# Third tile's weights loaded through POOL's queue, and the second block's last rows of x rounded before the first two evictions

## The chip, the cores and the metric

The kernel runs on one core of a Trainium2 chip. The metric is the device time of one execution in microseconds, as the median of several runs. The kernel before took 900.96 us (three runs, 900.55 to 901.79).

## What is computed

Two attention branches over one input x of 2048 positions by 448 features, in float32, 16 heads of 28 features each, mixed by a gate:

```python
def reference(A_x, A_wqkv, A_wo, B_x, B_wqkv, B_wo, gate_w):
    x = A_x
    g = _sigmoid((x * gate_w).sum(-1, keepdims=True))
    a = _A_ref(x, A_wqkv, A_wo)   # each position attends to itself and 7 earlier ones, 2 apart
    b = _B_ref(x, B_wqkv, B_wo)   # full attention: softmax(q k^T / sqrt(28)) v over all 2048 positions
    return g * a + (1 - g) * b
```

Each branch starts with a product of x with its 448 by 1344 matrix `wqkv` and ends with one with its 448 by 448 matrix `wo`. The change lies in the first microseconds of the first of these products.

## The kernel before

**Tiles and precision.** A float32 product is made of three products of rounded numbers: each operand is split into a rounded high part (ScalarE, a copy into the type float32r) and the rest (a subtraction on VectorE or GpSimd), and high times high, low times high and high times low are added up in PSUM. The names are `xh` and `xl` for x, `wh` and `wl` for weights, `raw`, `wr` and `wt` for weights as loaded, and `V` for x as loaded (the tile that later holds v serves as the landing place). x is laid out with its 448 features along the partitions, as three groups of 128 (`kt` 0 to 2) and a last group of 64 rows, the *tail* (`kt` 3), whose low part lies in the other 64 partitions of the same tile. It is cut into four blocks of 512 positions.

**The opening.** Queries and keys of the full attention are projected first, in tiles of 128 features by 512 positions. Tiles 0 and 1 take block 0 with two slices of the weights (`wa`, columns 128 to 383 of the set); tile 2 takes block 0 with a third slice (`wb`, the first 128 columns), which has loads of its own: `wr1` (384 rows, 192 KB, L413) and the tail half of `wt0` (twice 64 rows, 32 KB each, L414 through L234). Tile 3 is the first that takes block 1. Tiles 0 and 1 are interleaved so that TensorE can follow the arrival of the pieces (`FIRST`, L300); from tile 2 on a tile is eleven matmuls in the order of L298: four of high by high, four of high x by low weights, three of low x by high weights. Nine matmuls on zeros (L217) run ahead of all that.

**What sets the order.** The order of each engine's work is the order in which the code is written (a manual schedule). The loads of the opening are written at L408 to L419: the first weights and, through ScalarE's queue, the three groups of block 0; then, all through SyncE's queue, the tail of block 0, the tail half of the weights, `wr1`, the rest of the tail half, the tail of block 1 (L415), the three groups of block 1 (L416), block 2, the tails of blocks 2 and 3, block 3. Each DMA counts on one of eight semaphores in turn, and a DMA that reuses one waits for the DMA eight places earlier. GpSimd fills two key tiles with ones (L82) and then has nothing to do until the second weight set.

**ScalarE and VectorE in the opening.** After block 0 and its weights they split `wt0` and `wr1` for tile 2 (L437 to L439, through L228 and L229), evict tiles 0 and 1 from PSUM (L361 and L362), then split block 1 (`split_x(1)`, written behind tile 1 at L482): its tail first (L259, L260), and then its three groups (L228, L229). Evicted tiles are stored to DRAM (L99) and read back later.

**After the opening.** The projections of v and of the other branch follow, with the first pass of the full attention (S1: row maxima) mixed in between from tile 11 on; the main loop then runs over 16 groups of queries and heads by 16 key tiles, with the sliding attention on GpSimd and VectorE beside it; the output projection ends the kernel.

Of the kernel before, what the change touches and what calls it, by code (L numbers as in the profile page):

```python
# [25 lines left out]
def gated_mix_kernel(ctx: ExitStack, tc: tile.TileContext, xT, xn, gw, wA, wB, woAB, out):  # L26
    nc = tc.nc
# [61 lines left out]
    def ptile(name):  # L89
        if name[0] == "w":  # L90
            return pair(name)[:, 0, :]
        h = half.setdefault(name[:2], [])
        if not h:
            t = pair(name)
            h.extend((t[:, 1, :], t[:, 0, :]))
        return h.pop()
# [5 lines left out]
    def load_k(g, t, src, c=slice(0, S)):  # L102
        for h in range(4):
            r = D + 112 * g + DH * h
            dma_r(t[32 * h:32 * h + DH, c], src[r:r + DH, c])
# [114 lines left out]
    with tc.tile_pool(name="xp", bufs=1) as xp, tc.tile_pool(name="wp", bufs=2) as wp:  # L220
# [3 lines left out]
        def raw3():  # L224
            return wp.tile([128, 3, 450], F32, tag="raw", name="raw", bufs=2)

        def split(hi, lo, raw, eng=nc.vector):
            nc.scalar.activation(hi, raw, AF.Copy)  # L228
            eng.tensor_tensor(out=lo, in0=raw, in1=hi.bitcast(F32), op=ALU.subtract)  # L229


        def both(dst, src, eng=nc.sync):
            for h in (0, 64):
                eng.dma_start(dst[h:h + 64], src)  # L234
# [8 lines left out]
        def load_tails(b0, b1):  # L243
            nc.sync.dma_start(xst[HIGH[b0], b0:b1, 3, :], xT[384:448, 512 * b0:512 * b1].rearrange(
                "p (b c) -> p b c", c=512))
# [2 lines left out]
        LOW = [slice(64, 128)] * 2 + [slice(0, 64)] * 2  # L248
        HIGH = LOW[2:] + LOW[:2]

        def split_x(nb):
            r, t = xst[:, nb, 0:3, :], xst[:, nb, 3, :]
            tail = xh[nb][:, 3, :]
            o, i = LOW[nb], HIGH[nb]
            for kt in (3, 0, 1, 2) if nb == 1 else range(4):
                if kt < 3:
                    split(xh[nb][:, kt, :], xl[nb][:, kt, :], r[:, kt, :])
                else:
                    nc.scalar.activation(tail[i], t[i], AF.Copy)  # L259
                    nc.vector.tensor_tensor(out=tail[o], in0=t[i], in1=tail[i].bitcast(F32), op=ALU.subtract)  # L260
# [3 lines left out]
        def load_w(wi, tails=(False, True)):  # L264
            src, cols = WSRC[wi]
            if wi not in wraw:
                wraw[wi] = raw3(), wp.tile([128, 450], F32, tag="wt", name="wt"), sum(c1 - c0 for c0, c1 in cols) + 2 * (wi == GATE)
            r, t, _ = wraw[wi]
            for tail in tails:
                o = 0  # L270
                for c0, c1 in cols:
                    e = o + c1 - c0
                    if tail:
                        both(t[:, o:e], src[384:448, c0:c1])
                    else:
                        nc.sync.dma_start(r[:, :, o:e], src[0:384, c0:c1].rearrange("(k p) c -> p k c", p=128))
                    o = e

                if wi == GATE:
                    if tail:  # L280
                        both(t[:, o:o + 2], gw[0:2, 384:448].rearrange("i p -> p i"))
                    else:
                        for kt in range(3):
                            nc.sync.dma_start(r[:, kt, o:o + 2],
                                              gw[0:2, 128 * kt:128 * kt + 128].rearrange("i p -> p i"))

        def split_w(wi, kts):
            if wi not in wsets:
                wsets[wi] = [wp.tile([128, 4, 450], F32R, tag=g, name=f"{g}{wi}") for g in ("wh", "wl")]
            wh, wl = wsets[wi]  # L290
            r, t, n = wraw[wi]
            for kt in kts:
                split(wh[:, kt, :n], wl[:, kt, :n], r[:, kt, :n] if kt < 3 else t[:, :n], nc.gpsimd)
# [24 lines left out]
        def project(n):  # L318
            if n == 0:
                for m, p in FIRST:  # L320
                    product(m, p, None, p == (0, 0, 0), p == (0, 1, 3))
            elif n > 1:
                for i, p in enumerate(ORDER):
                    product(n, p, None, i == 0, i == len(ORDER) - 1)
# [4 lines left out]
        def project_halves(n, s1):  # L329
            if n % 2 == 0:  # L330
                for m in (n, n + 1):
                    low = (tiles[m][2] if tiles[m][1] == "qk" else tiles[m][-1] // 4) < 2
                    for half in range(2):
                        l = [p for p in ORDER if p != (0, 1, 3) or half == (0 if low else 1)]
                        l = [(m, product, (m, p, half, i == 0, i == len(l) - 1)) for i, p in enumerate(l)]
                        if s1[m - n]:
                            l[8:8] = [(m, s1_half, (1, half))]
                            l[2:2] = [(m, s1_half, (0, half))]
                        todo[half] += l
            while any(l and l[0][0] == n for l in todo):  # L340
                for l in todo:
                    if l:
                        _, f, x = l.pop(0)
                        f(*x)
# [61 lines left out]
        wr0, wt0, wr1 = raw3(), ptile("wt0"), ptile("wr1")  # L406
        wr1 = wr1[:, 0:384].rearrange("p (k c) -> p k c", k=3)
# [2 lines left out]
            load_x(0, kt, kt + 1, nc.scalar)  # L410
        load_tails(0, 1)
        both(wt0[:, 128:384], wB[384:448, 448:704])
        nc.sync.dma_start(wr1, wB[0:384, 0:128].rearrange("(k p) c -> p k c", p=128))  # L413
        both(wt0[:, 0:128], wB[384:448, 0:128])  # L414
        load_tails(1, 2)  # L415
        load_x(1)  # L416
        load_x(2)
# [41 lines left out]
        for n, t in enumerate(tiles):  # L459
            wi = t[0]  # L460
            for w in loads:
                if loads[w] == n:
                    load_w(w)
            for w in splits:
                i, k = (n - splits[w][0]) * splits[w][1], splits[w][1]
                if 0 <= i < 4:
                    split_w(w, range(i, i + k))
            if n in (3, 5):
                split_x((n + 1) // 2)
            if n < FULL:  # L470
                project(n)
            else:
                project_halves(n, [S1_START <= m < S1_START + 80 for m in (n, n + 1)])
            if t[1] == "qk":
                for m in {0: (), 1: (0, 1)}.get(n, (n,)):
                    qk_tile(m, *tiles[m][2:4])
            elif t[1] == "v":
                add_halves(n, V[:, t[2], :, 0:DH])
            else:
                a_tile(n, t[2], t[3])  # L480
            if n == 1:
                split_x(1)  # L482
            if n == 4:
                for t in QP[1]:
                    nc.scalar.activation(t, t0, AF.Copy)
            while fini and fini[0][0] <= n:
                fini.pop(0)[1]()
            if n in (2, 3):
                load_w(1, (n == 3,))
            if n == 3:  # L490
                load_qhi(0)
            if n in (3, 8):
                load_k(0, KH[0], qk_hi, slice(0, 1024) if n == 3 else slice(1024, S))
            if n == 16:
                for i in (1, 2):
                    nc.sync.dma_start(a_scr[i][:, 0:NJ, :].rearrange("c j e -> c (j e)").rearrange(
                        "c (a b) -> c a b", b=NJ), omg[0:8, None, :].to_broadcast([8, 56, NJ]))
            if n == 32:
                nc.gpsimd.memset(V[:, :, :, DH:], 1.0)
            if n == 22:  # L500
                load_k(1, KH[1], qk_hi)
            if n == 62:
                load_k(0, KL[0], qk_lo)
            if parts and parts[0][0] <= n:
                _, u, t = parts.pop(0)
                max_store(u, max_turn(t))
            if finished and n < len(tiles) - 3:
                u = finished.pop(0)
                parts.append((n + 3, u, max_parts(u)))
            if n == 64:  # L510
                gate = []
                for sgn, dst in ((-1.0, g_t), (1.0, omg)):
                    e = sp.tile([128, NJ], F32, name="ez")
                    nc.scalar.activation(e, zt, AF.Exp, scale=sgn)
                    nc.gpsimd.tensor_tensor(out=e, in0=e, in1=V[:, 0, :, DH], op=ALU.add)
                    gate.append((dst, e))
            if n in (66, 68):
                nc.vector.reciprocal(*gate.pop(0))
            if n == 70:
                nc.sync.dma_start(og_scr.rearrange("(j p) -> p j", j=NJ), omg)  # L520
            if n == 76:
                load_q(0)
# [183 lines left out]
    for c in range(8):  # L706
# [20 lines left out]
        n = 0  # L727
# [362 lines left out]
```

## Time and profile before

| | |
|---|---|
| median of three runs | 900.96 us (900.55 to 901.79) |
| the profiled execution: time, span | 900.95 us, 899.2 us |
| granted TensorE clock | 1.0 |
| busy in the span: PE, DVE, ACT, POOL | 892.3 us (99%), 739.0 us (82%), 643.1 us (72%), 639.7 us (71%) |
| DMA queues in use | q1 (SyncE), q10 (ScalarE), and two that fetch instructions |

The span runs from the first to the last instruction; the time of the execution has 1.75 us more around it. PE is TensorE's matmuls, PEld its weight loads, which overlap the matmuls, DVE is VectorE, ACT ScalarE, POOL GpSimd, and SPq SyncE's queue, which issues DMAs. In a row of a timeline stand the start in the span, the time covered (merged rows of one kind together), engine, line, operation, output and input, the count, and in brackets how long the engine had been idle and what ended that. The short names 128*128 and 128x512 are the shapes of the operands.

### The profile page before, as it was taken

How to read it: one execution, taken by the hardware profiler on the slowest of the kernel's cores; microseconds unless marked ns; L12 is line 12 of the kernel's file. 1: busy time of each engine (PE TensorE's matmuls, PEld its weight loads, DVE VectorE, ACT ScalarE, POOL GpSimd, SP SyncE). 2: the span in 40 equal slices, each digit the busy share in tenths (PEclk: the TensorE clock that was granted, in tenths of full speed). 3: DMA queues.
4: the chain of work that ended last, by engine and by line, in shares of the span. 5: the costliest groups of instructions: out<-in, count | busy, mean ns of one | idle time of the engine just before them, and what ended most of it. 6: DMA issues, size and time to landing. Idle time of an engine off the chain costs nothing.

```text
span 899.2 us, 20532 instructions
## 1 busy us (share of the span) xinstructions
PE 892.3 (99%) x8323; PEld 525.1 (58%) x8323; DVE 739.0 (82%) x961; ACT 643.1 (72%) x765; POOL 639.7 (71%) x506
## 2 busy tenths in 40 slices
PE   9999999999999999999999999999999999999998
PEld 6888999998954444444444444444444444434997
DVE  6588999998979999999999999989999999832220
ACT  7456434343378898988988989889889898897220
POOL 1499847464459689999999999999999698501000
PEclk9999999999999999999999999999999999999999
DMA  8877403559472341226225242352220322337691
GB/s 268 284 256 197 138 12 84 143 136 95 123 239 73 100 127 46 70 57 156 70 56 145 84 115 64 88 136 65 53 64 18 94 43 56 96 81 208 183 272 52
DMA packets 115975, 104.51 MB, mean 116 GB/s; under 512 B 77177, under 2 KB 84217, under 8 KB 115097
## 3 DMA queue, kind: packets, MB, share of 16 engines
q1 hardware_dynamic: 115448, 102.42, 42.6%
q8 instruction: 65, 1.06, 0.5%
q10 hardware_dynamic: 432, 0.79, 0.3%
q14 instruction: 30, 0.24, 0.1%
HBM read 62.20 MB, written 40.96 MB: 115 GB/s over the span
## 4 chain that ended last, share of the span: by engine, by line
PE 94%; POOL 2%; DMA 1%; ACT 1%; DVE 0%; issue 0%; SPq 0%; POOLq 0%; ACTq 0%
PE T L991 29%; PE av L957 26%; PE r L316 15%; PE r L311 8%; PE T L837 8%; PE r L148 5%; PE T L148 4%; DMA rbc<-rs 1%; POOL prod L670 1%; POOL oat L675 1%; DMA vt<-a_scr 0%; POOL prod L614 0%; PE r L217 0%; ACT P L996 0%; ACT raw L380 0%
## 5 line engine op out<-in xcount | busy, mean ns | idle before, releaser
L996 ACT ACTIVATE P<-T 128x1024 f32<-128x1024 f32 x512 | 496.8, 1023 | 60.4 <-PE T L991 58.4
L154 DVE TENSOR_REDUCE MX<-T 128x1 f32<-128x512 f32 x470 | 441.8, 953 | 34.2 <-PE T L148 18.2
L957 PE MATMUL av<-P,V 128*32 128x512 f32 x2048 | 272.7, 605 | 0.0
L991 PEld LDWEIGHTS T<-QH,KH 30*128 30x128 f32 x1024 | 92.2, 181 | 231.1 <-ACT P L996 197.0
L148 PE MATMUL T<-KH,QP 28*128 28x512 f32 x704 | 219.9, 455 | 0.1
L991 PE MATMUL T<-QH,KH 30*128 30x512 f32 x1024 | 212.1, 489 | 0.6 <-DVE MX L154 0.4
L170 DVE TENSOR_REDUCE MX<-r 128x2 f32<-128x1024 f32 x160 | 192.5, 1221 | 23.9 <-PE r L148 19.9
L991 PE MATMUL T<-QH,KL 28*128 28x512 f32 x1024 | 186.7, 395 | 0.0
L991 PE MATMUL T<-QL,KH 28*128 28x512 f32 x1024 | 184.5, 392 | 0.0
L614 POOL TENSOR_TENSOR prod<-qt,kt 128x896 f32<-128x896 f32 x64 | 135.4, 2116 | 5.5 <-DMA kt<-a_scr 5.4
L380 ACT ACTIVATE raw<-r 128x896 f32<-128x896 f32 (+1 forms) x64 | 58.9, 921 | 98.0 <-PE r L316 96.4
L148 PE MATMUL r<-KH,QP 64*128 64x512 f32 x320 | 105.6, 391 | 0.0
L675 POOL TENSOR_TENSOR oat<-oat,prod 128x896 f32<-128x896 f32 x48 | 101.3, 2110 | 2.0
L148 PEld LDWEIGHTS T<-KH,QP 28*128 28x128 f32 x704 | 86.0, 181 | 27.2 <-ACT P L996 19.5
L381 POOL TENSOR_TENSOR ast<-raw 128x448 f32<-128x448 f32 x48 | 55.4, 1154 | 59.2 <-ACT raw L380 51.7
L670 POOL TENSOR_TENSOR prod<-vt,L 128x896 f32<-128x896 f32 x56 | 95.3, 1701 | 0.2
L316 PE MATMUL r<-wh,xh 64*128 64x448 f32 (+1 forms) x512 | 93.7, 363 | 0.9 <-ACT raw L380 0.9
L991 PEld LDWEIGHTS T<-QL,KH 28*128 28x128 f32 x1024 | 94.5, 184 | 0.0
L991 PEld LDWEIGHTS T<-QH,KL 28*128 28x128 f32 x1024 | 93.2, 183 | 0.3
L957 PEld LDWEIGHTS av<-P,V 128*32 128x32 f32 x2048 | 40.3, 107 | 77.7 <-issue 65.3
L316 PEld LDWEIGHTS r<-wh,xh 64*128 64x128 f32 x512 | 74.0, 185 | 4.0 <-ACT raw L380 1.3
L316 PE MATMUL r<-wh,xl 64*128 64x448 f32 (+1 forms) x384 | 73.6, 364 | 0.0
(114 smaller groups left out, 1115.6 us busy)
## 6 DMA issues: line engine op xcount, KB each, us to landing
a_scr<-ast SPq DMA_DIRECT2D x24, 448.0 KB
qk_hi<-qkh SPq DMA_DIRECT2D x24, 256.0 KB
qk_lo<-qkh SPq DMA_DIRECT2D x24, 256.0 KB
rbc<-rs SPq DMA_DIRECT2D x64, 64.0 KB
QP<-qk_hi SPq DMA_DIRECT2D x64, 56.0 KB
KL<-qk_lo SPq DMA_DIRECT2D x16, 224.0 KB
QH<-qk_hi SPq DMA_DIRECT2D x64, 56.0 KB
QL<-qk_lo SPq DMA_DIRECT2D x64, 56.0 KB
```

The lines of the kernel that those rows point to most:

```text
L148: nc.tensor.matmul(bank, qhis[u][h % 2][r, 128 * qs:128 * qs + 128], KH[u // NB % 3][r, 512 * kc:512 * kc + 512], start=True, stop=True)
L154: i = nc.vector.tensor_reduce(MX[:, n % NMX:n % NMX + k], bank, axis=X, op=ALU.max)
L170: nc.vector.tensor_reduce(m, PM[k], axis=X, op=ALU.max)
L311: nc.tensor.matmul(bank, ws[c][rows, k, t[4]:t[4] + 128], x, start=first, stop=last)
L316: nc.tensor.matmul(bank[:, 0:cols], x, ws[c][rows, k, 0:cols], start=first, stop=last)
L614: nc.gpsimd.tensor_tensor(out=p, in0=qt[c], in1=kvt["k", c % 2][:, HALO - DIL * w:HALO - DIL * w + NJ, :], op=ALU.mult)
L670: nc.gpsimd.tensor_tensor(out=dst.rearrange("p j (h d) -> p j h d", d=DH), in0=kvt["v", c % 2][:, HALO - DIL * w:HALO - DIL * w + NJ, :].r ...
L675: nc.gpsimd.tensor_tensor(out=ows[c % 2][:, :, 0:56] if w == W - 1 else oat[c], in0=oat[c], in1=oat[c, w], op=ALU.add)
L837: writes(bank, nc.tensor.matmul(bank[:, :D], src, wo[c][k], start=(first and k == ks[0] and i == 0), stop=(last and k == ks[-1] and i == 2)))
L957: nc.tensor.matmul(av[32 * h:32 * h + 32, :], V[:, kt, 4 * g + h, :], tiles_[h], start=(kt == 0), stop=(kt == NJ - 1), skip_group_check=True)
L991: nc.tensor.matmul(bank[a], (KH[g % 3], KH[g % 3], KL[g % 2])[t][r, ks], (qh, ql, qh)[t][r, :], start=(t == 0), stop=(t == 2))
L996: e = nc.scalar.activation(p, one if a == "2" else mine, AF.Exp, scale=SCALE).ins
```

## The change

It does two things.

The loads of tile 2's weights, `wr1` and the last two pieces of `wt0`, are issued by GpSimd (`nc.gpsimd`) and no longer by SyncE. They stand where they stood in the code, so in GpSimd's order they come behind the two fills of the key tiles, and in SyncE's order the tail and groups of block 1 and everything behind them move up three places.

`split_x` takes the groups that it is to split. The tail of block 1 is split at the end of step 0 of the tile loop, ahead of the evictions of tiles 0 and 1, which are written in step 1; the three groups stay behind these evictions.

```diff
-        def split_x(nb):
+        def split_x(nb, kts=range(4)):
             r, t = xst[:, nb, 0:3, :], xst[:, nb, 3, :]
             tail = xh[nb][:, 3, :]
             o, i = LOW[nb], HIGH[nb]
-            for kt in (3, 0, 1, 2) if nb == 1 else range(4):
+            for kt in kts:
...
         both(wt0[:, 128:384], wB[384:448, 448:704])
-        nc.sync.dma_start(wr1, wB[0:384, 0:128].rearrange("(k p) c -> p k c", p=128))
-        both(wt0[:, 0:128], wB[384:448, 0:128])
+        nc.gpsimd.dma_start(wr1, wB[0:384, 0:128].rearrange("(k p) c -> p k c", p=128))
+        both(wt0[:, 0:128], wB[384:448, 0:128], nc.gpsimd)
         load_tails(1, 2)
         load_x(1)
...
                 project_halves(n, [S1_START <= m < S1_START + 80 for m in (n, n + 1)])
+            if n == 0:
+                split_x(1, (3,))
             if t[1] == "qk":
...
             if n == 1:
-                split_x(1)
+                split_x(1, range(3))
```

SyncE's queue at the start of the program, as the difference of the two orders (`V` is x as loaded, with 64 partitions for a tail and 128 for groups; `wr_192` and `wt_191` are the weights of tile 2):

```order
 L409 DMA raw<-in_wB 128x256 x3
 L244 DMA V<-in_xT 64x512
 L234 DMA wt_191<-in_wB 64x256 x2
-L413 DMA wr_192<-in_wB 128x3x128
-L234 DMA wt_191<-in_wB 64x128 x2
 L244 DMA V<-in_xT 64x512
 L240 DMA V<-in_xT 128x3x512 x2
```

The three DMAs of tile 2's weights are gone from this queue, and block 1's tail and groups follow the first pieces of `wt0` directly.

GpSimd's queue at the same place, as it stands now (`KH` are the key tiles; `wl_404` and `wh_403` belong to the second weight set, which comes much later):

```order
L82 MEMSET KH_151 128x2048
L82 MEMSET KH_152 128x2048
L413 DMA wr_192<-in_wB 128x3x128
L234 DMA wt_191<-in_wB 64x128 x2
L229 TENSOR_TENSOR wl_404<-raw,wh_403 128x384 x3
```

The three DMAs stand behind the second fill and ahead of the first subtraction of the second weight set.

ScalarE around the first evictions (`qkh` is a tile as evicted from the PSUM banks `r`; `xh_181` is block 1's high part):

```order
 L228 ACTIVATE wh_188<-wr_192 128x3x128
 L228 ACTIVATE wh_188<-wt_191 128x128
+L259 ACTIVATE xh_181<-V 64x512
 L361 ACTIVATE qkh<-r_128 128x512
 L361 ACTIVATE qkh<-r_132 128x512
-L259 ACTIVATE xh_181<-V 64x512
 L228 ACTIVATE xh_181<-V 128x512 x3
 L361 ACTIVATE qkh<-r_136 128x512
```

The rounding of block 1's tail has moved ahead of the evictions of tiles 0 and 1. VectorE's subtraction of the tail (L260) moves in the same way ahead of its two subtractions for these tiles (L362). On TensorE nothing moves.

## The prediction

> **What bounds the kernel now.** I read the page's busy times first, then the chain of waits, then the waits of the matmuls, to see whether a microsecond won or lost in the opening reaches the end.
>
> ```profile
> span 899.2 us, 20532 instructions
> PE 892.3 (99%) x8323; PEld 525.1 (58%) x8323; DVE 739.0 (82%) x961; ACT 643.1 (72%) x765; POOL 639.7 (71%) x506
> PE 94%; POOL 2%; DMA 1%; ACT 1%; DVE 0%; issue 0%; SPq 0%; POOLq 0%; ACTq 0%
> ...
> PE r L217 <- DVE omg L213: 1.4, 1, 1.4
> PE r L316 <- ACT raw L380: 0.9, 1, 0.9
> PE T L991 <- DVE MX L154: 0.4, 1, 0.4
> PE T L991 <- ACT P L996: 0.2, 1, 0.2
> ```
>
> PE carries 94% of the chain that ended last, and outside the start its matmuls wait 0.9 + 0.4 + 0.2 = 1.5 us in all. Nothing later has slack worth naming that could swallow a shift of the opening, so a shift there is passed on to the end nearly one for one. What the change can win is therefore whatever PE stands still in the opening. The timeline of the weight loads and of the matmuls shows where that is: the weight load waits and the matmuls behind it start late.
>
> ```profile
> 9.92 0.30 PEld L311 LDWEIGHTS r<-xh,wh 128*128 128x128 f32 x2 [0.31 <-ACT wh L228]
> 13.42 0.19 PEld L311 LDWEIGHTS r<-xh,wh 128*128 128x128 f32 x1 [0.20 <-ACT xh L228]
> 13.94 0.19 PEld L311 LDWEIGHTS r<-xh,wh 128*128 128x128 f32 x1 [0.33 <-ACT xh L228]
> 14.46 0.30 PEld L311 LDWEIGHTS r<-xh,wh 128*128 128x128 f32 x2 [0.34 <-ACT xh L228]
> ...
> 10.95 1.09 PE L311 MATMUL r<-xh,wh 128*128 128x512 f32 x4
> 11.88 1.09 PE L311 MATMUL r<-xh,wl 128*128 128x512 f32 x4
> 12.80 0.86 PE L311 MATMUL r<-xl,wh 128*128 128x512 f32 x3
> 13.50 1.70 PE L311 MATMUL r<-xh,wh 128*128 128x512 f32 x4
> 15.03 1.09 PE L311 MATMUL r<-xh,wl 128*128 128x512 f32 x4
> ```
>
> Tile 2 runs from 10.95, tile 3 from 13.50. Four undisturbed matmuls take 11.88 - 10.95 = 0.93 us, but the first four of tile 3 take 15.03 - 13.50 = 1.53. So **0.60 us** of PE's time is lost there, to ACT's rounding of block 1. ACT's own timeline says why it is late:
>
> ```profile
> 8.76 0.40 ACT L228 ACTIVATE wh<-wt 128x256 fp32r<-128x256 f32 x1
> 9.07 0.51 ACT L228 ACTIVATE wh<-wr 128x384 fp32r<-128x384 f32 x1
> 9.48 0.30 ACT L228 ACTIVATE wh<-wt 128x128 fp32r<-128x128 f32 x1
> 10.92 1.09 ACT L361 ACTIVATE qkh<-r 128x512 fp32r<-128x512 f32 x2 [1.14 <-PE r L311]
> 11.89 0.62 ACT L259 ACTIVATE xh<-V 64x512 fp32r<-64x512 f32 x1
> 12.74 1.67 ACT L228 ACTIVATE xh<-V 128x512 fp32r<-128x512 f32 x3 [0.23 <-DMA V<-in_xT]
> ```
>
> It idles 1.14 us before the evictions, then has evictions, tail and the three groups in a row, and it waits 0.23 us more for block 1 to land. The change puts the tail into the 1.14 us and brings block 1 forward.
>
> **Part one, ACT's order.** Starts of neighbours here lie about 0.10 closer than their durations (0.51 long, 0.41 to the next), so the tail takes 0.52 and the 128 columns of `wt` take 0.20. The evictions cannot start before 10.92 (they wait for PE) and last 11.89 - 10.92 = 0.97 to the next start; then the three groups need 1.67. Before, they ended at 12.74 + 1.67 = 14.41 and PE's next group began at 15.03, 0.62 later. With X as the start of the 9.48 row, the rest follows: evictions at the later of 10.92 and X + 0.72, and tile 3's second group at T = max(14.43, X + 0.72 + 0.97 + 1.67 + 0.62) = max(14.43, X + 3.98). If X stays at 9.48, T is 14.43 and all 0.60 us is won. It is won up to X = 10.45, gone at X = 11.05, and beyond that each microsecond of X costs one.
>
> On DVE the tail's subtraction moves ahead of the evictions' subtractions:
>
> ```profile
> 10.64 0.29 DVE L229 TENSOR_TENSOR wl<-wt,wh 128x128 fp32r<-128x128 f32 x1
> 11.55 1.29 DVE L362 TENSOR_TENSOR qkh<-r,qkh 128x512 fp32r<-128x512 f32 x2 [0.62 <-ACT qkh L361]
> 12.87 0.68 DVE L260 TENSOR_TENSOR xh<-V,xh 64x512 fp32r<-64x512 f32 x1
> ```
>
> It would run from 10.93 to 11.61, so the evictions on DVE start 0.06 later. What waits for them are stores and tile 4, which needs tile 0's PSUM bank eleven matmuls after tile 3's start, at 13.50 + 11 x 0.93 / 4 = 16.1; the bank is free by 11.61 + 1.29 / 2 = 12.3. This cover of 3.8 us makes the cost nothing; without it the 0.06 would be on PE.
>
> **Part two, the queues.** The SP and POOL timelines:
>
> ```profile
> 2.71 2.42 SPq L234 DMA_DIRECT2D wt<-in_wB  x2
> 5.18 0.59 SPq L413 DMA_DIRECT2D wr<-in_wB  x1
> 5.82 1.17 SPq L234 DMA_DIRECT2D wt<-in_wB  x2
> 7.03 0.59 SPq L244 DMA_DIRECT2D V<-in_xT  x1
> 7.92 0.91 SPq L240 DMA_DIRECT2D V<-in_xT  x2
> ...
> 1.25 3.54 POOL L82 MEMSET KH<- 128x2048 f32 x2
> 28.24 2.01 POOL L229 TENSOR_TENSOR wl<-raw,wh 128x384 fp32r<-128x384 f32 x2 [23.45 <-ACT wh L228]
> ```
>
> SP loses 0.59 + 1.17 us of issue. Block 1's tail goes out at 5.18 instead of 7.03 and its groups at about 5.82 instead of 7.92, provided that the semaphores of the new rotation are free; the one for the groups is that of the second weight piece, which ACT had used at the latest at 6.36. Block 1 then took 12.74 - 7.92 = 4.82 us to land, so now 10.6, ahead of the groups' new start at 11.89: the 0.23 us wait is gone with 1.3 us to spare. The tail would have to land by 10.45 and has 5.3 us for it.
>
> POOL is free from 1.25 + 3.54 = 4.79 until 28.24, so its three issues hold up nothing of its own. What they cost is X: no transfer in this trace is issued by POOL, so I bound it. From below: POOL issues as fast as SP, 1.76 us, and the last lands as on SP, at most 9.48 - 6.99 = 2.49 us after its issue ended (ACT used it then without a wait). X = 4.79 + 1.76 + 2.49 = 9.04: free. From above: each issue costs as much as one of POOL's fills, 3.54 / 2 = 1.77 and 5.31 in all, and landing takes block 1's 4.82: X = 14.92, T = 18.90, a loss of 3.87. I take SP's time stretched as POOL's subtraction is against DVE's. That is 2.01 / 2 = 1.0 for 128x384 on POOL and 0.56 on DVE for the same shape:
>
> ```profile
> 10.17 0.56 DVE L229 TENSOR_TENSOR wl<-wr,wh 128x384 fp32r<-128x384 f32 x1
> ```
>
> A factor of 1.8: 3.2 us of issue, X = 4.79 + 3.2 + 2.49 = 10.5, T = 14.5, and 0.5 us is won. This is an estimate, and nearer to the low end because a queue that only issues has no 2048 columns to write.
>
> **A price on the way: block 0's last group.** It comes through ACT's queue and PE follows it closely:
>
> ```profile
> 5.83 0.63 ACT L429 ACTIVATE xh<-V 128x512 fp32r<-128x512 f32 x1 [0.83 <-DMA V<-in_xT]
> 7.39 0.63 ACT L429 ACTIVATE xh<-V 128x512 fp32r<-128x512 f32 x1 [0.63 <-DMA V<-in_xT]
> 6.00:6.75 0.75, 0.75 (x5) 0.56 (x4) 0.42 (x2) 0.75 (x2) 0.00 (x0) 1.00 1.03 309
> 8.25:9.00 0.75, 0.75 (x4) 0.49 (x4) 0.75 (x2) 0.75 (x3) 0.00 (x0) 1.00 0.58 137
> ```
>
> In the last two columns of the stretches (share of the DMA engines, GB/s), the DMA engines are full at 6 us and at 0.58 at 8.25 to 9, so the bulk of block 1 moves into a gap. But 7.39 - 5.83 = 1.56 us for this group was a share of two queues, and a third queue could stretch it to 1.5 times that: 0 to 0.78 us on PE's path from 8.38 on. POOL's first transfer comes hardly earlier than SP's did, so I take 0.2. Then T = max(14.43 + 0.2, 14.5) = 14.63, and **0.4 us** remains. The profiled execution took 900.95 us, the median run 900.96: both give 900.55, rounded to 900.6.
>
> **Rivals.**
>
> *The first transfers through POOL are slow (slower).* Place: between 4.79 and X. It decides from X + 3.98 = 15.03 + 1.8, so X = 12.85, 8.1 us after POOL is free against my 5.7; the upper bound above gives 904.8. For it: no row shows such a transfer, and POOL's only other work there is 1.8 times as slow as DVE's. Against it: three small transfers, 256 KB. The Trainium skill, "GPSIMD Engine Reference", section "2.1 Instruction dispatch", says that the first call of a freshly loaded routine on that engine takes about 6 us more; if that held here X would be 16.5 and the time, as an estimate, about 906.4, but no row shows whether the routine counts as freshly loaded.
>
> *POOL's issue and DVE's work exclude each other (slower).* From 4.68 DVE works on SBUF almost without a break:
>
> ```profile
> 4.68 0.43 DVE L426 CAST xh<-V 128x512 fp32r<-128x512 f32 x1 [3.23 <-DMA V<-in_xT]
> 6.49 0.69 DVE L431 TENSOR_TENSOR xl<-V,xh 128x512 fp32r<-128x512 f32 x1 [0.33 <-ACT xh L429]
> 8.06 0.69 DVE L431 TENSOR_TENSOR xl<-V,xh 128x512 fp32r<-128x512 f32 x1 [0.54 <-ACT xh L429]
> ```
>
> Were POOL held until the gap before 8.06, at 7.52, X would be 10.5 + 2.73 = 13.23, T 17.2 and the time 903.1. Against it: the fills ran up to 4.79 beside the cast, and its 0.43 us is not drawn out beside the 0.69 of a subtraction of the same shape. The Trainium skill, "SBUF — State Buffer", section "SBUF: two separate sides", says that a transfer issued from GpSimd stands still while DVE runs a copy in its two-port mode; only the cast at 4.68 is such a copy, so by that rule X moves to about 10.8 and the time to about 900.7, as an estimate: no other verdict.
>
> *Block 0's last group pays it all back.* With the full 0.78, T is 15.2 and the time 901.1. For it: the DMA engines are full at that point.
>
> *More than the wait goes.* Faster by over 0.2% needs 1.8 us. Even with the wait at 9.92 (0.31) and all 1.5 us of later matmul waits the sum is 0.60 + 0.31 + 1.5 = 2.4, a time of 898.5; I see no link from the opening to those.
>
> **How the numbers follow.** About 0.2%, 1.8 us, is what a measurement of this kernel can tell from no change. My forecast (0.2 to 0.6 us won, 900.6) has a chance of 0.47; the payback by block 0, 0.15; slow transfers through POOL, 0.22; POOL and DVE excluding each other, 0.10; more than the wait, 0.06. Faster by over 0.2%: 0.06. Within 0.2%: 0.47 + 0.15 = 0.62. Slower: 0.22 + 0.10 = 0.32. The forecast's own range is 900.2 to 901.2. The range of 8 in 10 takes in the payback, the exclusion and the nearer half of the slow transfers: 900.0 to 904.0.
>
> **What would show it.** Right: three issues on POOL right behind 4.79 that together take about 3 us; the 128-column rounding of `wt` on ACT starting by 10.5; the tail's rounding directly behind it and before the evictions; no wait for DMA before block 1's groups; tile 3's four matmuls in about 0.93 us. Wrong: an idle of ACT before `wr` or `wt` that a DMA ended, PE standing in tile 2 instead of tile 3, longer DVE subtractions between 5 and 9 us, or ACT's wait for block 0's last group grown beyond 0.63. The prediction fails if X passes 12.85 or if PE's stall turns up again later, in the S1 tiles.

## The result, and the profile after

The change makes the kernel **slower by 2.0 us**: 902.51 us (median of 22 runs) against 900.55 us, a ratio of 1.0022 with a 95% interval of 1.0016 to 1.0028. Forecast was a gain of 0.2 to 0.6 us; the range of 900.0 to 904.0 holds the time, the direction is wrong. The profiled execution of the change took 902.40 us with a span of 900.6, 1.4 longer than that of before.

The loss sits in the opening. This is the chain of work that ended last, in order of time, in the kernel after (start, length, what):

```profile
1.31 3.49 POOL KH L82 x2
4.80 0.89 POOL wr L413
5.69 0.52 POOL wt L234
6.21 6.00 DMA wt<-in_wB
...
12.29 0.32 ACT wh L228
12.62 0.04 issue
12.66 2.50 PE r L311 x9
...
15.71 20.57 PE r L311 x99
```

Before, this chain ran through PE from 1.45 us on. Now it leaves PE and runs through GpSimd's fills, its issues, and then 6.00 us in one of the two 32 KB pieces of `wt`. The timeline of ScalarE, GpSimd and SyncE's queue shows the same (rows answer to those shown of before):

```profile
4.75 0.94 POOL L413 DMA_DIRECT2D wr<-in_wB  x1
5.69 1.05 POOL L234 DMA_DIRECT2D wt<-in_wB  x2
...
5.40 0.60 SPq L244 DMA_DIRECT2D V<-in_xT  x1
6.04 1.14 SPq L240 DMA_DIRECT2D V<-in_xT  x2
...
10.12 0.53 ACT L228 ACTIVATE wh<-wr 128x384 fp32r<-128x384 f32 x1 [0.46 <-DMA wr<-in_wB]
12.29 0.31 ACT L228 ACTIVATE wh<-wt 128x128 fp32r<-128x128 f32 x1 [1.65 <-DMA wt<-in_wB]
12.51 0.62 ACT L259 ACTIVATE xh<-V 64x512 fp32r<-64x512 f32 x1
13.03 1.06 ACT L361 ACTIVATE qkh<-r 128x512 fp32r<-128x512 f32 x2
13.99 1.67 ACT L228 ACTIVATE xh<-V 128x512 fp32r<-128x512 f32 x3
```

The three issues take 1.99 us in all (4.75 to 6.74), but ScalarE can start on the last pieces only 12.29 - 6.74 = 5.55 us after that. ScalarE waits 0.46 us for `wr` and 1.65 us for `wt`, and all that stands behind them moves. The wait for block 1's groups has gone, as intended (13.99 has no idle). On PE:

```profile
11.34 0.85 PE L311 MATMUL r<-xh,wh 128*128 128x512 f32 x3
12.66 0.50 PE L311 MATMUL r<-xh,wh 128*128 128x512 f32 x1 [0.46 <-ACT wh L228]
12.99 1.10 PE L311 MATMUL r<-xh,wl 128*128 128x512 f32 x4
14.66 1.77 PE L311 MATMUL r<-xh,wh 128*128 128x512 f32 x4
16.27 1.09 PE L311 MATMUL r<-xh,wl 128*128 128x512 f32 x4
```

PE now stands in tile 2, before its fourth matmul, and again in tile 3, whose second group starts at T = 16.27 instead of 15.03. With X = 12.29 the sum of the prediction gives X + 3.98 = 16.27: its arithmetic was right and its X, 10.5, was not. From there on the chain is as before (20.57 us for the next 99 matmuls in both).

### The profile page after: what moved, and what is told of

Read it like the earlier page. It is cut to its first block, busy times and chain, and to the rows that moved or that the text cites. A ratio compares the mean times of both kernels' runs of the same rounds, so it can differ in the third digit from the quotient of the medians.

```text
span 900.6 us, 20537 instructions
## 1 busy us (share of the span) xinstructions
PE 892.7 (99%) x8323; PEld 530.5 (59%) x8323; DVE 739.2 (82%) x961; ACT 643.3 (71%) x765; POOL 641.9 (71%) x509
## 3 DMA queue, kind: packets, MB, share of 16 engines
q8 instruction: 65, 1.06, 0.5%
## 4 chain that ended last, share of the span: by engine, by line
PE 93%; POOL 4%; DMA 1%; ACT 1%; DVE 0%; issue 0%; SPq 0%; POOLq 0%; ACTq 0%
PE T L993 29%; PE av L959 26%; PE r L316 15%; PE T L839 8%; PE r L311 7%; PE r L148 4%; PE T L148 4%; POOL prod L616 1%; POOL prod L672 1%; POOL oat L677 1%; DMA wt<-in_wB 1%; POOL prod L621 0%; POOL KH L82 0%; ACT P L998 0%; DVE MX L154 0%
## 5 line engine op out<-in xcount | busy, mean ns | idle before, releaser
L148 PE MATMUL r<-KH,QP 64*128 64x512 f32 x320 | 102.1, 392 | 0.0
L316 PE MATMUL r<-wh,xh 64*128 64x448 f32 (+1 forms) x512 | 91.5, 363 | 1.0 <-ACT raw L380 1.0
```

The source lines that it names most:

```text
L148: nc.tensor.matmul(bank, qhis[u][h % 2][r, 128 * qs:128 * qs + 128], KH[u // NB % 3][r, 512 * kc:512 * kc + 512], start=True, stop=True)
L316: nc.tensor.matmul(bank[:, 0:cols], x, ws[c][rows, k, 0:cols], start=first, stop=last)
```

## The experiments

In each trace X is the start of ScalarE's 128-column rounding of `wt`, T the start of tile 3's second group of matmuls. The ratio is that of a run's times to those of before on the same chip, with its 95% interval. The opening moves by some tenths from one execution to the next, so the two kernels were profiled once more (the last two runs), each in a single execution that has no ratio of its own. Not in the table is a run with two probe loads, which lies far behind the opening.

| run | X | T | ratio to before |
|---|---|---|---|
| before / once more | 9.48 / 9.16 | 15.03 / 14.75 | 1 |
| the change / once more | 12.29 / 13.01 | 16.27 / 16.99 | 1.0022 [1.0016, 1.0028] |
| tail alone | 9.86 | 15.39 | 0.9997 [0.9988, 1.0006] |
| GpSimd's queue alone | 12.72 | 16.69 | 1.0018 [1.0009, 1.0026] |
| bulk of x held back | 9.32 | 15.48 | 1.0011 [1.0001, 1.0021] |
| block 1 on GpSimd's queue | 12.13 | 16.10 | 1.0015 [1.0006, 1.0024] |
| all on SyncE, block 1 first | 11.95 | 15.92 | 1.0011 [1.0001, 1.0020] |
| issues before the fills | 10.86 | 17.81 | 1.0021 [1.0011, 1.0030] |
| issues between the fills | 10.85 | 17.62 | 1.0026 [1.0016, 1.0037] |
| issues first, fills held | 10.90 | 15.51 | 1.0009 [1.0000, 1.0018] |
| only the tail on GpSimd's queue | 9.93 | 14.67 | 0.9994 [0.9985, 1.0004] |

**The two parts apart.** The tail's early rounding with all loads on SyncE's queue:

```diff
-        nc.gpsimd.dma_start(wr1, ...)
-        both(wt0[:, 0:128], wB[384:448, 0:128], nc.gpsimd)
+        nc.sync.dma_start(wr1, ...)
+        both(wt0[:, 0:128], wB[384:448, 0:128])
```

> Only the second part: the tail of block 1 is rounded before the evictions, all loads stay on SyncE's queue. Every theory puts the loss into the loads of tile 2's weights, so X, the start of the 128-column rounding of wt on ACT, stays at 9.48 and no DMA is waited for there. Block 1's groups still land at about 12.5, so they are rounded from 12.5 instead of 12.74 and tile 3's second group of matmuls starts at about 14.8 instead of 15.03: 0.2 us faster than before, which the times will hardly tell. If instead the moved tail itself costs time (it holds up the evictions or the subtractions on VectorE), that group starts after 15.03.

No gain and no loss that the times can tell: the ratio's interval holds 1. The 0.2 us expected in T did not come; T is 15.39 (PE began this execution's third group of x 0.3 us later). The tail does run in ScalarE's idle time, but block 1 has not landed when the evictions are done, and ScalarE waits 0.78 us for it instead of 0.23:

```profile
10.32 0.64 ACT L259 ACTIVATE xh<-V 64x512 fp32r<-64x512 f32 x1 [0.16 <-DMA V<-in_xT]
11.23 1.09 ACT L361 ACTIVATE qkh<-r 128x512 fp32r<-128x512 f32 x2 [0.28 <-PE r L311]
13.10 1.67 ACT L228 ACTIVATE xh<-V 128x512 fp32r<-128x512 f32 x3 [0.78 <-DMA V<-in_xT]
```

By itself this part only changes what is waited for. The other part alone:

```diff
-            if n == 0:
-                split_x(1, (3,))
...
-                split_x(1, range(3))
+                split_x(1, (3, 0, 1, 2))
```

> Only the first part: tile 2's weights go through GpSimd's queue, the tail stays behind the evictions. If the whole loss comes from the late landing of these weights, X is 12.3 as with the whole change, ACT has the same work in another order behind it, tile 3's second group starts at 16.2 to 16.3 and the kernel is 1.2 to 2 us slower than before. If the moved tail had a share in the loss, it starts earlier than 16.1.

X is 12.72 and T = 16.69, X + 3.97. The whole loss is in the loads.

**The path, or the company.** Theory A: the weights land late because the bulk of x now moves beside them. Theory B: a transfer issued by GpSimd takes about 5 us to land in any case. First, the change with the bulk of x (block 1 and all of x behind it) held back: two one-column fills on VectorE, which the loads must follow, stand behind the second low part of the weights.

```diff
+            if kt == 1:
+                nc.vector.memset(xst[HIGH[1], 1, 3, 0:1], 0.0)
+                nc.vector.memset(xst[:, 1, 0:3, 0:1], 0.0)
+                load_tails(1, 2)
+                load_x(1)
...
```

> The whole change, but the loads of block 1 and all x behind it are held back until VectorE has done the second low part of the weights (about 7.5 us), as late as SyncE issued them before. Theory A, competition: the weights through GpSimd's queue land late because the bulk of x now runs beside them; without it they land as on SyncE's queue, X is 9.5 to 10.3. Theory B, the path itself: a transfer that GpSimd issues takes some 5 us to land whatever runs beside it; X stays at 12 or later. In both, block 1 lands at about 13, so tile 3's second group starts at about 15.3 by A and at 16.2 or later by B.

```profile
5.68 1.05 POOL L234 DMA_DIRECT2D wt<-in_wB  x2
7.60 0.47 SPq L244 DMA_DIRECT2D V<-in_xT  x1
8.16 1.06 SPq L240 DMA_DIRECT2D V<-in_xT  x2
...
9.32 0.30 ACT L228 ACTIVATE wh<-wt 128x128 fp32r<-128x128 f32 x1
...
13.19 1.67 ACT L228 ACTIVATE xh<-V 128x512 fp32r<-128x512 f32 x3 [1.10 <-DVE qkh L362]
```

The same three issues from GpSimd, at the same time, and X is 9.32 with no wait: theory B falls. Now block 1 is the late one (13.19; the wait is put down to VectorE, but its loads alone were held back), and 13.19 + 1.67 + 0.62 = 15.48 is T. The second test was meant to measure the path by itself: in the kernel before, the same two pieces of 64 rows by 512 bytes are loaded far from the opening, once by each queue, and ScalarE waits for them.

```diff
+            if n in (50, 54):
+                q = sp.tile([128, 128], F32, name="probe")
+                both(q, wB[384:448, 0:128], nc.gpsimd if n == 50 else nc.sync)
+                nc.scalar.activation(q, q, AF.Copy)
```

> The kernel before, with two probes in a stretch with little DMA traffic: the same two pieces of 64 rows by 512 bytes, once through GpSimd's queue and some steps later through SyncE's, each followed by a copy on ScalarE that waits for it. Theory A: from the end of the issue to the start of the copy both queues take about the same, 1.5 to 2.5 us. Theory B: 4 us or more on GpSimd's queue, about 2 on SyncE's. The time of the whole is longer by a few us and tells nothing.

```profile
146.85 1.22 POOL L234 DMA_DIRECT2D probe<-in_wB  x2
150.61 0.31 ACT L507 ACTIVATE probe<-probe 128x128 f32<-128x128 f32 x1 [5.08 <-DMA probe<-in_wB]
162.03 1.46 SPq L234 DMA_DIRECT2D probe<-in_wB  x2
165.44 0.31 ACT L507 ACTIVATE probe<-probe 128x128 f32<-128x128 f32 x1 [5.09 <-DMA probe<-in_wB]
```

From the end of the issues to the copy: 150.61 - 148.07 = 2.5 us on GpSimd's queue, 165.44 - 163.49 = 2.0 on SyncE's. The stretches were not quiet: before each probe SyncE issued a store of 448 KB (at 146.79 and 161.61), and the DMA engines were full (a share of 1.03 from 148 to 149 us, 1.06 from 163 to 164). GpSimd's packets moved from 149.2 on, when the store was nearly through (149.4); SyncE's probe stood behind the store in its own queue. So the 0.5 us between the two is no clean price of the path. What holds is an upper bound: the path through GpSimd takes at most 2.5 us here, so of the 5.55 us of the change at least 3 are company.

**Which queue, or which order.** If company is the cause, it should hold with the roles swapped, the weights on SyncE and block 1 on GpSimd:

```diff
-        load_tails(1, 2)
-        load_x(1)
+        load_tails(1, 2, nc.gpsimd)
+        load_x(1, eng=nc.gpsimd)
```

> The two queues swap roles: tile 2's weights stay on SyncE's queue as before, the tail and the groups of block 1 go through GpSimd's queue behind the fills, and the tail is rounded early. Theory A1: whatever is small loses beside a bulk on another queue; then the weights on SyncE's queue land late now, X above 11. Theory A2: it is GpSimd's transfers that lose beside SyncE's; then X stays at 9.5 to 10.2 and it is block 1 that is held up, by block 2 on SyncE's queue, tile 3's second group after 15.0. If nobody is held up, that group starts at 14.4 to 14.7.

```profile
12.13 0.31 ACT L228 ACTIVATE wh<-wt 128x128 fp32r<-128x128 f32 x1 [1.09 <-DMA wt<-in_wB]
```

X is 12.13: theory A1. The weights on SyncE's own queue, issued as early as before, now land as late as GpSimd's did. And with no second queue at all, block 1 ahead of the weights on SyncE's:

```diff
+        load_tails(1, 2)
+        load_x(1)
         nc.sync.dma_start(wr1, ...)
         both(wt0[:, 0:128], wB[384:448, 0:128])
-        load_tails(1, 2)
-        load_x(1)
```

> No transfer through GpSimd: all on SyncE's queue, but block 1's tail and groups ahead of tile 2's weights, with the tail rounded early. If the loss of the change is only that 0.9 MB of block 1 is now ahead of the weights, X comes out as late as in the change, 11.5 to 13, and the time is 1 to 2.5 us above before. If X is 10.5 or less, GpSimd's queue adds something of its own beside the bulk.

```profile
11.46 0.52 ACT L228 ACTIVATE wh<-wr 128x384 fp32r<-128x384 f32 x1 [2.65 <-DMA wr<-in_wB]
11.95 0.31 ACT L228 ACTIVATE wh<-wt 128x128 fp32r<-128x128 f32 x1
```

X is 11.95. So the delay needs neither queue in particular: putting the weights on GpSimd's queue took them off SyncE's and let 0.9 MB of block 1, and x behind it, go beside them, which delays them about as much as putting block 1 in front of them.

**Cures tried.** GpSimd issues the weights before its fills, and in a second version between the two:

```diff
-    for t in KH:
-        init_kh(t)
...
         both(wt0[:, 0:128], wB[384:448, 0:128], nc.gpsimd)
+        for t in KH:
+            init_kh(t)
```

> The whole change, but GpSimd issues the weights of tile 2 before its two fills, at about 1.3 us. Theory A: they land before the bulk of block 1 moves (X 9.3 to 9.9, set by ACT's order alone), the tail fills ACT's idle time and block 1 lands by 11.9, so tile 3's second group starts at 14.4 to 14.9; 256 KB more beside block 0 may delay block 0 by up to 0.7 us, which then counts against it. Time 0 to 0.7 us below before, or up to 0.3 above if block 0 pays. A theory in which the path itself is slow by 5 us would still land them in time here, so this run tells only whether the early issue is a cure.

> The whole change, but the three issues stand between GpSimd's two fills, at about 3.0 us, 1.75 us earlier than in the change. Theory A: the transfers are ahead of block 1's groups, but share with block 0: X 9.5 to 10.4, tile 3's second group at 14.4 to 14.9, 0.1 to 0.6 us faster than before. If earlier issue only means waiting longer, X stays above 11.5 and the loss of the change stays.

Both miss. X falls to 10.86 and 10.85, but T is 17.8 and 17.6, and the time is as bad as with the change (1.0021 and 1.0026; the intervals overlap). A new stall stands ahead of all this: VectorE's cast of block 0 takes 2.47 us instead of 0.43 (timeline of the version with the issues between the fills):

```profile
3.94 1.05 POOL L233 DMA_DIRECT2D wt<-in_wB  x2
4.98 1.82 POOL L82 MEMSET KH<- 128x2048 f32 x1
...
4.62 2.47 DVE L426 CAST xh<-V 128x512 fp32r<-128x512 f32 x1 [3.17 <-DMA V<-in_xT]
...
7.24 0.70 PE L310 MATMUL r<-xh,wh 128*128 128x512 f32 x2 [1.77 <-DVE xh L426]
```

The fill ends at 6.80 and the cast at 7.09. To test that it is the fill, the next run issues first and holds both fills until the cast is done (a one-column fill on VectorE, written behind the cast, which they must follow):

```diff
-    for t in KH:
-        init_kh(t)
...
         nc.vector.tensor_copy(xh[0][:, 0, :], r[:, 0, :])
+        nc.vector.memset(KH[0][:, 0:1].bitcast(F32), 1.0)
+        for k in KH:
+            init_kh(k)
```

> The early issue of the weights through GpSimd (before the fills) again, but the fills wait until VectorE's cast at 4.7 us is done (a one-column fill on VectorE that they must follow). If the 2 us in the two runs with earlier issue came from the fills and the cast excluding each other, the cast takes 0.43 us again, tiles 0 and 1 start at 5.4 to 5.6, X is 9.9 to 10.9 (the last pieces of block 0 still land late beside block 1) and tile 3's second group starts at 14.4 to 14.9: at or up to 0.6 us below before. If the cast stays at 2.4 us, its cause is another, the three issues for instance.

The cast (first row below) takes 0.43 us again with the three issues as early as in the first of the two versions, so it was the fills. T is 15.51, later than expected. Tile 3 itself no longer waits, but tiles 0 and 1 do: block 0's second group lands late (rounded at 6.38 after 1.39 us of idle, where the kernel before had 5.83), and so does its tail. The early weights and block 1 run beside them, which is the likely cause; no run separates it:

```profile
4.72 0.43 DVE L424 CAST xh<-V 128x512 fp32r<-128x512 f32 x1 [3.27 <-DMA V<-in_xT]
...
6.38 0.63 ACT L430 ACTIVATE xh<-V 128x512 fp32r<-128x512 f32 x1 [1.39 <-DMA V<-in_xT]
9.53 0.63 ACT L436 ACTIVATE xh<-V 64x512 fp32r<-64x512 f32 x1 [0.76 <-DMA V<-in_xT]
```

The last version leaves the weights on SyncE's queue ahead of block 1 and gives only the 128 KB tail of block 1 to GpSimd:

```diff
-        nc.gpsimd.dma_start(wr1, ...)
-        both(wt0[:, 0:128], wB[384:448, 0:128], nc.gpsimd)
-        load_tails(1, 2)
+        nc.sync.dma_start(wr1, ...)
+        both(wt0[:, 0:128], wB[384:448, 0:128])
+        load_tails(1, 2, nc.gpsimd)
```

> A version meant to win: tile 2's weights stay on SyncE's queue ahead of block 1, only the 128 KB tail of block 1 goes through GpSimd's queue behind the fills, and it is rounded early. Theory A (what stands behind the bulk lands late, whichever queue): the weights are ahead of the bulk, X 9.5 to 10.2; block 1's groups are issued about 0.9 us earlier than before and land at about 11.7; tile 3's second group starts at 14.4 to 14.7, 0.3 to 0.6 us faster than before, below what the times can tell. If the tail on GpSimd's queue is itself held up, ACT waits for it after X and that group starts after 15.0.

```profile
12.22 1.68 ACT L228 ACTIVATE xh<-V 128x512 fp32r<-128x512 f32 x3
...
13.74 1.09 PE L311 MATMUL r<-xh,wh 128*128 128x512 f32 x4
14.67 1.09 PE L311 MATMUL r<-xh,wl 128*128 128x512 f32 x4
```

Tile 3's four matmuls take 14.67 - 13.74 = 0.93 us: the stall that the change was after is gone, and T is the earliest of all. The time, 0.9994 of before, is not told apart from before. Its gain in T, 0.1 to 0.4 us against the two profiles of before, is below what the times can show.

> The kernel before, profiled once more, to see how far the opening moves from one execution to the next: X at 9.3 to 9.9, tile 3's second group at 14.9 to 15.4.

> The whole change, profiled once more, for the same reason: X at 12.0 to 12.8, tile 3's second group at X + 4.0.

Before came out earlier than expected (X 9.16, T 14.75), the change later (X 13.01, T 16.99 = X + 3.98). The mean of two executions each puts T at 16.63 against 14.89, a loss of 1.7 us, within the 1.4 to 2.5 us that the ratio's interval gives.

## Why the prediction was wrong

**What bounds the kernel, and that the opening is passed on to the end: right.** The loss in T, 1.7 us, and the loss in time, 2.0, agree.

**The stall of 0.60 us and its cause: right.** With the weights in time, block 1 earlier and the tail early, it is gone (only the tail on GpSimd's queue).

**The sum T = X + 3.98: right.** It gives T to 0.01 us in the five runs with X over 11 (12.29, 12.72, 12.13, 11.95 and 13.01). Below that, as foreseen, T hangs on other things: block 1's landing where it is late, PE's own pace where tiles 0 and 1 are.

**The issue on GpSimd: mis-sized, on the safe side.** 3.2 us were taken, 1.99 measured.

**The landing: the step that failed.** "The last lands as on SP, at most 9.48 - 6.99 = 2.49 us after its issue ended" carried a duration from a queue in which these pieces stood ahead of block 1 into one in which they run beside it. Measured were 5.55 and 6.3 us (13.01 - 6.74), even beyond the 4.82 taken as the upper bound, which is block 1's own. The prediction asked what the bulk does to block 0's last group, and priced that at 0 to 0.78 us; it did not ask it of the weights themselves, and it read the stretch from 8.25 on as a gap that block 1 could fill for nothing. The packets show what happens there. GpSimd's queue is q0 in the table of queues (packets, MB, share of the DMA engines' time), here of the change from 10 to 12.2 us:

```profile
q1 hardware_dynamic: 393, 0.77, 98.9%
q0 software_dynamic: 27, 0.03, 4.6%
```

and here of the run with the bulk held back, from 6 to 10 us:

```profile
q1 hardware_dynamic: 322, 0.40, 44.2%
q0 software_dynamic: 128, 0.26, 25.5%
```

In the second all 128 packets of the weights are through within that stretch. In the change 27 of them are still trickling in after 10 us, among 393 packets of x. GpSimd's first packets move between 6.5 and 7 us in both runs; the last ones move before 8.5 us with the bulk held back, and after 11 us in the change. The Trainium skill, "DMA: Bandwidth & Descriptors", section "Queues, rings and completion order", says that each DMA engine takes turns between the queues packet by packet; the first table is compatible with that, since neither queue shuts the other out, but it does not show the turns themselves.

**The rivals.** The one of slow transfers through GpSimd had the sign, at 0.22, and the wrong mechanism: the first issue took 0.94 us, without block 1 beside them the pieces landed within 2.5 to 2.6 us of their issue (the probes, and 9.32 - 6.73 with the bulk held back), and its threshold, X = 12.85, was met by one of two profiles. So it was luck that the range held the time: its upper end had been set for this rival and for the exclusion. The payback by block 0's last group was small: it was rounded at 7.79 and 7.29 instead of 7.39 and 7.06. The exclusion of GpSimd's issues and VectorE did not show (the cast takes 0.43 us beside an issue, the subtractions 0.69), but the fills and the cast do exclude each other. The row that the prediction held against an exclusion, the cast's 0.43 us beside fills up to 4.79, could not show it: in the two versions that show it the cast ends 0.28 to 0.29 us after the fill, here at about 5.07, and the cast had its 0.43 us to run until 5.11 anyway.

## What to carry to other kernels

Moving a transfer to another queue also moves up everything that stood behind it in the old one; before counting the issue time as won, ask which of the transfers that are waited for next now shares the DMA engines with the bulk that was brought forward. In an opening like this one, with the DMA engines full for most of it, what counts is the order in which bytes are wanted, and a second queue gives that order away. Of what was moved to GpSimd's queue here (tile 2's weights, the whole of block 1, block 1's tail), only the 128 KB tail, which is wanted after the weights, left without harm.

## What the runs showed of the hardware

**A fill on GpSimd blocks a cast on VectorE from SBUF to SBUF.** The cast ended 0.28 to 0.29 us after the end of the last fill in both versions where they met for long (fills to 6.80 and 7.01, casts to 7.09 and 7.29), and in the change once more, where it started at 4.50 under a fill that ran to 4.81, it took 0.58 us and ended at 5.08. This is the lock that the prediction put on the issues. The Trainium skill, "SBUF — State Buffer", section "Who interferes with whom", says that VectorE in its two-port mode and GpSimd wait for each other for a whole instruction, whichever is first; the traces agree in that the cast stands still for a whole fill, and show that a fill, which reads nothing, is enough. They do not bear out that the first one goes ahead: in one version the cast's row starts at 4.62, before the fill's at 4.98, and in the other a second fill goes ahead of the cast that had stood since 4.86. VectorE's subtractions are not held: beside the held fills (5.24 to 8.80) they took 0.69 and 0.42 us, as in the kernel before.

**After a gap of 1.8 us TensorE had half its clock for 3.4 us, after one of 2.05 us it had not.** In the version with the issues between the fills PE waited 1.77 us for the cast. Busy times by stretch follow; the third number from the end is the granted clock:

```profile
5.50:7.50 2.00, 0.26 (x1) 0.29 (x2) 1.97 (x2) 0.94 (x2) 1.31 (x1) 1.00 1.12 293
7.50:9.50 2.00, 2.00 (x7) 1.36 (x7) 2.00 (x5) 1.46 (x3) 0.00 (x0) 0.75 1.05 228
9.50:11.50 2.00, 2.00 (x6) 1.54 (x6) 1.94 (x5) 1.39 (x4) 0.00 (x0) 0.50 1.04 358
11.50:13.50 2.00, 2.00 (x10) 1.60 (x9) 1.06 (x3) 0.16 (x1) 0.00 (x0) 0.90 1.06 380
```

The gap itself and the slow stretch behind it together made T 2.7 us later than the mean of before. In stretches of a quarter of a microsecond the clock stood at 0.50 from about 8.5 to 11.9 us here, from about 8.85 to 12.25 behind a gap of 1.82 us in the version with the issues before the fills, and from about 152.65 to 156.1 behind a gap of 2.51 us at the first probe: 3.4 us each time. But PE stood for 1.53 us before its fourth matmul of tile 2 in the change once more, and for 2.05 us at the second probe, and the clock stayed at 1.00 both times. So the length of the gap alone does not decide; what does was not tried.
